# Turning one batch's queries with a DMA transpose instead of TensorE

## The chip, the cores and the metric

The kernel runs on one core of a Trainium2 chip. A core has TensorE (PE: matmuls, with weight loads counted apart as PEld), VectorE (DVE), ScalarE (ACT), GpSimd (POOL) and SyncE (SP), which here only issues DMA transfers. Each engine works through its own instructions in order and waits on semaphores for the others. The metric is the device time of one execution in microseconds (us); the kernel before takes 230.7 us, the median of three runs from 230.65 to 230.78.

## The reference, cut to what matters

Attention over keys and values that are averaged in groups of eight, then a maxout layer and an output matmul. There are 8 batches, 8 heads, 576 positions and 64 channels a head; 4608 tokens of 512 channels enter the second part.

```python
k_p = k.reshape(B, H, Sp, 8, D).mean(axis=3)       # 72 pooled keys per head
v_p = v.reshape(B, H, Sp, 8, D).mean(axis=3)
scores = scale * np.matmul(q, k_p.transpose(0, 1, 3, 2))
attn = softmax(scores)                             # written out in the reference
x = np.matmul(attn, v_p)                           # -> (B*S, H*D), heads side by side
h = np.maximum(np.maximum(x @ w1, x @ w2), x @ w3)
out = h @ w_out
```

## The kernel before

The kernel interleaves the attention of batch b with the matmuls of the second part for tokens that are already there. The second part goes in blocks of 512 tokens. A block is a list of short pieces of TensorE work, its slots: first the hidden layer (`hidden`), then the output (`project`, two slots for 128 tokens each). After each slot a plan can insert steps of a batch's attention. Batches are counted from 0, so "the third batch" is batch 2.

The steps that matter here:

```python
# loads, issued by GpSimd; the pool ld has two buffers for each of q, k and v
    def after(loads, first):          # the loads also wait for this instruction
        ...
    def load_q(b):
        qbs[b] = ld.tile([128, 4, NG, D], BF16, name="qb", tag="qb")
        src = q[b].rearrange("h s d -> (h s d)").rearrange(
            "(hp p t d) -> p hp t d", hp=4, p=128, t=NG)
        n = 2 if b == 0 else 4
        for i in range(0, 4, n):
            nc.gpsimd.dma_start(out=qbs[b][:, i:i + n], in_=src[:, i:i + n])

# adding up groups of eight keys or values on GpSimd (or VectorE)
    def fold(e, t, out, dtype=F32):
        part, n = t.shape[:2]
        f = const.tile([part, n, 4, D], dtype, name="half" if dtype == F32 else "halfh",
                       tag="half" if dtype == F32 else "k16")
        e.tensor_tensor(out=f, in0=t[:, :, 0:4, :], in1=t[:, :, 4:8, :], op=ALU.add)
        e.tensor_tensor(out=f[:, :, 0:2, :], in0=f[:, :, 0:2, :], in1=f[:, :, 2:4, :],
                        op=ALU.add)
        e.tensor_tensor(out=out, in0=f[:, :, 0, :], in1=f[:, :, 1, :], op=ALU.add)

# turning queries on TensorE: transposes into PSUM (tag TR has one buffer), then a copy
    def turn_q(b, n0, n1, evac, tag):
        if b not in qTs:
            qTs[b] = sb2.tile([128, 2 * NG, 128], BF16, name="qT", tag="qT")
        pqt = psum([128, n1 - n0, 128], BF16, name="pqt", tag=tag[0],
                       bufs=tag[1])
        qf = qbs[b].rearrange("p hp t d -> p (hp t d)")
        for n in range(n0, n1):
            nc.tensor.transpose(pqt[:, n - n0, :], qf[:, 128 * n:128 * n + 128],
                                ident)
        evac(out=qTs[b][:, n0:n1, :], in_=pqt)

# turning keys: three transposes, then four copies that spread the heads into the kz tiles
    def turn_k(b):
        pkt = keys(b, ATT if len(pools) < 3 else SC)
        for par, evac in enumerate((nc.vector.tensor_copy, nc.scalar.copy)):
            for odd in range(2):
                (evac if b > 2 else nc.vector.tensor_copy)(
                    out=kz_all[b % 2][par][64 * par:64 * par + 64, :, 0:Sp].rearrange(
                         "p h (r i t) -> p h r i t", i=3, t=2)[:, :, :, :, odd],
                     in_=pkt[64 * odd:64 * odd + 64].rearrange("p i (h r) -> p h r i", r=12))

    def do(b, steps):                 # the plan's steps, by letter
            if name[0] in "qQ":       # a quarter of the queries, by TensorE
                turn_q(b, *QS[i], ... nc.scalar.copy, TR)    # QS: 5, 5, 4 and 4 transposes
            elif name[0] == "T":      # all queries of a batch, by one DMA transpose
                qTs[b] = sb2.tile([128, 2 * NG, 128], BF16, name="qT", tag="qT")
                nc.sync.dma_start_transpose(
                    out=qTs[b], in_=qbs[b].rearrange("p hp t d -> p (hp t d)"))
            elif name[0] == "k":
                turn_k(b)
            elif name[0] == "s": ...  # scores of head i: two matmuls (even and odd kz), then exp
            elif name[0] == "v": ...  # attention times values for a chunk of tokens
            elif name[0] == "x": ...  # turning the result into xT
```

The hidden layer's pieces take three PSUM buffers in turn. Of two pieces the first is read by ScalarE (`t`), the second by VectorE (`hT`, the maximum of both). Blocks 0 and 1 begin with twelve half-width pieces (slots 0 to 11); from slot 12 on they are 512 wide.

```python
    def hidden_part(n, jc, c0, c1, hT):
        col = slice(NB * n + c0, NB * n + c1)
        for wi in range(1, 3):
            pw = psum([128, c1 - c0], F32, name=f"pw{wi}", tag="pw", bufs=3)
            for kc in range(KCH):
                mm = nc.tensor.matmul(pw, w_sb[wi][:, kc, bass.ts(jc, 128)],
                                      xT[:, kc, col],
                                      start=(kc == 0), stop=(kc == KCH - 1))
            mms.append(mm)
            if wi == 1:
                t = sb2.tile([128, c1 - c0], F16, name="t0", tag="t0")
                nc.scalar.activation(out=t, in_=pw, func=FT.Relu)
            else:
                nc.vector.tensor_tensor(out=hT[:, jc, c0:c1], in0=t, in1=pw,
                                        op=ALU.max)
            yield
```

The output's pieces end in a copy on ScalarE into `osb` (five buffers) and two stores issued by SP:

```python
# [cut from project(n): matmuls with wm and wo]
                    nc.scalar.copy(out=osb[:, c], in_=po)
                for u in range(2):
                    b, g = divmod(2 * m + u, NG)
                    dst = out[S * b:S * b + S, :].rearrange("(r g) c -> r g c", g=NG)
                    (nc.scalar if last and u else nc.sync).dma_start(
                        out=dst[:, GS[g], c], in_=osb[64 * u:64 * u + 64, c])
```

Block 0, what GpSimd gets after it, block 1's plan, and what GpSimd gets at its first slot:

```python
    def block(n, plan, parts, folds=()):

        for slot, _ in enumerate(part for stage in parts for part in stage(n)):
            if slot == 0 and n > 0:
                pool_work(n, mms[-1])
            for b, steps in plan.get(slot, ()):
                if b < B:
                    do(b, steps)
            if folds and slot in FOLDS:
                next(folds.pop(0))

    fold_v(1)
    block(0, {0: [(0, "v2")], 1: [(0, "v3")], 3: [(0, "x2 x3 w1 v4")], 6: [(0, "x4 d1")], 9: [(0, "w2")], 10: [(0, "d2")], 11: [(0, "w3")], 12: [(0, "w4")], 14: [(0, "w5 z")],
              17: [(1, "K")], 24: [(1, "q0 k")], 25: [(1, "q1")],
              26: [(1, "s0 q2")], 27: [(1, "s1 s2")], 28: [(1, "s3 Q3")],
              29: [(1, "s4 s5")], 30: [(1, "s6 s7")], 31: [(1, "v0")],
              32: [(1, "v1 x0")], 33: [(1, "X1 v2 v3")]}, (hidden, project))
    load_k(3, nc.gpsimd)
    load_v(3, nc.gpsimd)
    load_q(3)
    fold_k(2, nc.gpsimd)
    fold_v(2)

    def plan1():
        return {1: [(1, "x2")], 2: [(1, "v4")], 3: [(1, "x3")],
                5: [(1, "x4")],
                6: [(2, "k")], 7: [(2, "q0")], 9: [(2, "q1")], 11: [(2, "q2 s0")],
                12: [(2, "s1 q3")], 13: [(2, "s2")], 14: [(2, "s3")], 15: [(2, "s4"), (3, "T")],
                16: [(2, "s5")], 18: [(2, "s7")],
                19: [(2, "v0")],
                20: [(2, "v1 x0")], 21: [(2, "v2 x1")], 22: [(2, "v3 x2")],
                23: [(2, "v4 x3")], 24: [(2, "x4"), (4, "T")], 17: [(2, "s6")]}

# [cut: plan(n) for the later blocks, with "T" two batches ahead]
    FOLDS_OF = {1: "k3 v3", 2: "k4 v4 k5", 3: "v5 k6 v6", 4: "k7 v7"}

    def pool_work(n, mm):

        if n + 3 < B:
            if n == 1:
                load_q(4)
            after([load_k(n + 3, nc.gpsimd)], mm)
            load_v(n + 3, nc.gpsimd)
            if n > 1:
                load_q(n + 3)
        for name in FOLDS_OF.get(n, "").split():
            if name[0] == "k":
                fold_k(int(name[1]), nc.gpsimd)
            else:
                fold_v(int(name[1]))
```

So batches 0, 1 and 2 have their queries turned by TensorE, batches 3 to 7 by a DMA transpose that SP issues. `load_q(4)` stands ahead of the folds of batch 3 in GpSimd's order.

Of the kernel before, what the change touches and what calls it, by code (L numbers as in the profile page):

```python
# [14 lines left out]
def kernel(  # L15
# [11 lines left out]
    nc = tc.nc  # L27
# [37 lines left out]
    kts, vts, qbs, kps, qTs, ets = {}, {}, {}, {}, {}, {}  # L65

    def after(loads, first):
        for x in loads:
            tc.add_manual_dep(x.ins, first.ins.name, mybir.DependencyInfo(
                mybir.DependencyClass.Sync, mybir.DependencyReason.DATA),  # L70
                reason="weights first")
# [22 lines left out]
    def load_q(b):  # L94
        qbs[b] = ld.tile([128, 4, NG, D], BF16, name="qb", tag="qb")
        src = q[b].rearrange("h s d -> (h s d)").rearrange(
            "(hp p t d) -> p hp t d", hp=4, p=128, t=NG)
        n = 2 if b == 0 else 4
        for i in range(0, 4, n):
            nc.gpsimd.dma_start(out=qbs[b][:, i:i + n], in_=src[:, i:i + n])  # L100

    w_sb = [const.tile([128, KCH, DFF], F16, name=f"mw{wi}", tag=f"mw{wi}")
            for wi in range(3)]
# [19 lines left out]
    for sign in (1, -1):  # L123
        nc.gpsimd.affine_select(
            out=pick, in_=pick, compare_op=ALU.is_ge, fill=0.0, base=7 * (sign < 0),
            pattern=[[sign, 6], [-8 * sign, 128]], channel_multiplier=6 * sign)
    for i in range(3):
        load_w(slice(256 * i, 256 * i + 256))
    nc.gpsimd.dma_start(
        out=wo_sb, in_=moe_w_out.rearrange("(jc p) c -> p jc c", p=128))  # L130
# [25 lines left out]
    def new_kp(b):  # L156
        kps[b] = sb2.tile([96, 6, D], BF16, name="kp", tag="kp")

    def fold_k(b, e, i0=0, i1=6):
        if b not in kps:  # L160
            new_kp(b)
        fold(e, kts[b][:, i0:i1], kps[b][:, i0:i1], F16 if e is nc.vector else F32)

    def fold_v(b):
        fold(nc.gpsimd, vts[b], vp_all[:, b, :, 0:D])
# [48 lines left out]
    def new_et(b):  # L214
        ets[b] = sb2.tile([Sp, H, S], F16, name="et", tag="et")
# [20 lines left out]
    def turn_x(b, c0, keep, xn, tag, evac=nc.scalar.copy):  # L236
        if b > 2:
            g0 = S * b + c0
            nc.sync.dma_start_transpose(
                out=xT[:, :, g0 + keep:g0 + 128],  # L240
                in_=xn.rearrange("p g h d -> p (g h d)")[keep:128])
            return
        pxt = psum([128, KCH, 128], F16, name="pxt", tag=tag[0], bufs=tag[1])
        for kc in range(KCH):
            nc.tensor.transpose(
                pxt[:, kc, :],
                xn[:, kc // 2, 2 * (kc % 2):2 * (kc % 2) + 2, :], identh)
        g0 = S * b + c0
        evac(out=xT[:, :, g0 + keep:g0 + 128], in_=pxt[:, :, keep:128])  # L249
# [23 lines left out]
    PW = ("pw", 3)  # L273

    QS = ((0, 5), (5, 10), (10, 14), (14, 18))
    xns, mms = {}, []

    def do(b, steps):

        for name in steps.split():
            i = int(name[1:] or 0)
            if name[0] in "qQ":
                turn_q(b, *QS[i], nc.vector.tensor_copy if name[0] == "Q"
                       else nc.scalar.copy, TR)
            elif name[0] == "T":
                qTs[b] = sb2.tile([128, 2 * NG, 128], BF16, name="qT", tag="qT")
                nc.sync.dma_start_transpose(
                    out=qTs[b], in_=qbs[b].rearrange("p hp t d -> p (hp t d)"))  # L290
            elif name[0] == "k":
                turn_k(b)
            elif name[0] == "K":
                fold_k(b, nc.vector)
            elif name[0] == "s":
                if i == 0:
                    new_et(b)
                (scores if len(pools) < 3 else scores_flat)(b, i)
            elif name[0] == "d":
                sub_w(i)  # L300
            elif name[0] == "z":
                for par in range(2):
                    nc.vector.memset(kz_all[1][par], 0.0)
            elif name[0] == "w":
                turn_w(i, nc.scalar.copy if i % 2 else nc.vector.tensor_copy)
            elif name[0] == "v":
                xns[b, i] = values(b, CHUNKS[i][0])
            else:
                turn_x(b, *CHUNKS[i], xns[b, i], TR if b == 1 else ATT,
                       nc.vector.tensor_copy if name[0] == "X" else nc.scalar.copy)  # L310
# [4 lines left out]
    def sub_w(i, j0=0, j1=2, wi=(1, 2)):  # L315

        part = slice(256 * i + 128 * j0, 256 * i + 128 * j1)
        for t in [w_sb[w] for w in wi]:
            nc.vector.tensor_tensor(out=t[:, :, part], in0=t[:, :, part],  # L319
                                    in1=w_sb[0][:, :, part], op=ALU.subtract)  # L320

    def turn_w(jc, evac):
        pwt = psum([128, KCH, 128], F16, name="pwt", tag=TR[0], bufs=TR[1])
        for kc in range(KCH):
            nc.tensor.transpose(pwt[:, kc, :], w_sb[0][:, kc, bass.ts(jc, 128)], identh)
        evac(out=w1T[:, jc, :], in_=pwt.rearrange("p k c -> p (k c)"))
# [171 lines left out]
    def block(n, plan, parts, folds=()):  # L498

        for slot, _ in enumerate(part for stage in parts for part in stage(n)):  # L500
            if slot == 0 and n > 0:
                pool_work(n, mms[-1])
            for b, steps in plan.get(slot, ()):
                if b < B:
# [9 lines left out]
              32: [(1, "v1 x0")], 33: [(1, "X1 v2 v3")]}, (hidden, project))  # L514
    load_k(3, nc.gpsimd)
    load_v(3, nc.gpsimd)
    load_q(3)
    fold_k(2, nc.gpsimd)
    fold_v(2)


    def plan1():
        return {1: [(1, "x2")], 2: [(1, "v4")], 3: [(1, "x3")],
                5: [(1, "x4")],
                6: [(2, "k")], 7: [(2, "q0")], 9: [(2, "q1")], 11: [(2, "q2 s0")],
                12: [(2, "s1 q3")], 13: [(2, "s2")], 14: [(2, "s3")], 15: [(2, "s4"), (3, "T")],
                16: [(2, "s5")], 18: [(2, "s7")],
                19: [(2, "v0")],
                20: [(2, "v1 x0")], 21: [(2, "v2 x1")], 22: [(2, "v3 x2")],
                23: [(2, "v4 x3")], 24: [(2, "x4"), (4, "T")], 17: [(2, "s6")]}  # L530
# [11 lines left out]
    def pool_work(n, mm):  # L542

        if n + 3 < B:
            if n == 1:
                load_q(4)
            after([load_k(n + 3, nc.gpsimd)], mm)
            load_v(n + 3, nc.gpsimd)
            if n > 1:
# [293 lines left out]
```

The softmax here doesn't subtract the row's maximum and nothing guards it: scores larger than these inputs give would overflow.

## Time and profile before

| what | before |
|---|---|
| time, median of three runs | 230.7 us |
| span of the profiled run | 229.0 us |
| TensorE busy | 219.8 us |
| GpSimd busy | 140.0 us |
| block 1, start to end on TensorE | 51.45 to 77.51 us |
| query transposes by TensorE (L182) | 54, 219 ns long in the median |
| query transposes by DMA (L289) | 5, landing 3.9 to 7.4 us after issue |

Times in the profile are us from the start of the span. A line such as "56.00 0.44 PE L182 MATMUL pqt<-ident,qb ... x5" gives start, length, engine, line of the kernel, operation, result and operands, and how many instructions were merged. Square brackets tell how long the engine was idle before, and what released it. Matmuls overlap in the pipeline, so a group's cost is read from the starts.

### The profile page before, as it was taken

Reading aid. Unit: us, or ns where it says so; the run is one execution under the profiler, and the core shown is the slowest. Engines: PE = TensorE matmul, PEld = TensorE weight load, DVE = VectorE, ACT = ScalarE, POOL = GpSimd, SP = SyncE. Lnnn points to the kernel's source line nnn. Section 1 sums busy time; section 2 is a strip of 40 time slices with the busy share of each in tenths; the row PEclk is TensorE's granted clock in tenths of the full one; section 3 lists DMA queues with packets and bytes.
Section 4 is the critical chain, followed back from the end, with each engine's and each line's share of the span. In section 5 each row is a group of like instructions: output and inputs, shape, how many; then the busy total and the mean of one; then the engine's idle time right before and its main releaser. Section 6 shows DMA issues by size and latency. Waiting matters only on the chain.

```text
span 229.0 us, 4411 instructions
## 1 busy us (share of the span) xinstructions
PE 219.8 (96%) x1686; PEld 134.9 (59%) x1687; DVE 130.5 (57%) x246; ACT 122.6 (54%) x221; POOL 140.0 (61%) x115
## 2 busy tenths in 40 slices
PE   7888999999999999999999999999999999999992
PEld 2477645568655545544554455455677667786682
DVE  3668876048426423632363236368578887897830
ACT  2277425756864586238623852683776435465330
POOL 7975201999959999999999759900343443920020
PEclk9999999999999999999999999999999999999999
DMA  6999999999569999986998799941421534301326
GB/s 172 208 197 197 211 202 208 194 177 225 106 110 216 221 161 212 159 194 119 223 153 199 127 218 189 190 110 24 92 53 40 121 71 87 84 11 46 76 68 183
DMA packets 47157, 33.52 MB, mean 146 GB/s; under 512 B 27104, under 2 KB 41888, under 8 KB 47136
## 3 DMA queue, kind: packets, MB, share of 16 engines
q0 software_dynamic: 16944, 16.98, 46.0%
q1 hardware_dynamic: 30032, 16.13, 32.2%
q8 instruction: 13, 0.21, 0.4%
q10 hardware_dynamic: 160, 0.13, 0.2%
q14 instruction: 8, 0.07, 0.1%
HBM read 34.60 MB, written 9.44 MB: 192 GB/s over the span
## 4 chain that ended last, share of the span: by engine, by line
PE 88%; DVE 6%; ACT 3%; issue 2%; DVEq 0%; ACTq 0%
PE pw L346 23%; PE po L395 18%; PE po L391 11%; PE pA L733 7%; PE psc L207 6%; PE pav L255 4%; PE pC L733 3%; PE wm L413 3%; PE pm L333 2%; PE oA L670 2%; PE pB L733 2%; DVE kz L198 2%; PE pqt L182 2%; DVE xn L263 2%; ACT kz L198 2%
## 5 line engine op out<-in xcount | busy, mean ns | idle before, releaser
L346 PE MATMUL pw<-xT,mw 128*128 128x512 f16 (+1 forms) x336 | 73.1, 349 | 0.4 <-ACT xT L249 0.2
L395 PE MATMUL po<-mwo,hT 128*128 128x512 f16 (+1 forms) x198 | 46.8, 373 | 0.0
L354 DVE TENSOR_TENSOR hT<-t,pw 128x512 f16<-128x512 f16 (+1 forms) x42 | 25.5, 610 | 36.7 <-ACT et L212 22.3
L346 PEld LDWEIGHTS <-mw 128*128 128x128 f16 x336 | 31.6, 98 | 21.5 <-DVE mw L319 0.6
L400 ACT COPY osb<-po 128x512 f32<-128x512 f32 (+1 forms) x32 | 18.5, 579 | 41.2 <-PE po L395 41.1
L212 ACT ACTIVATE et<-psc 72x576 f16<-72x576 f32 (+2 forms) x54 | 35.2, 660 | 7.1 <-PE psc L207 6.9
L151 POOL TENSOR_TENSOR half<-vt 72x2048 f32<-72x2048 f16 x7 | 28.4, 4060 | 14.1 <-DMA vt<-in_v_dram 13.7
L391 PE MATMUL po<-wm,xT 128*128 128x512 f16 (+1 forms) x132 | 33.0, 372 | 0.3 <-ACT osb L400 0.3
L352 ACT ACTIVATE t<-pw 128x512 f16<-128x512 f32 (+1 forms) x42 | 22.5, 537 | 13.4 <-PE pw L346 11.6
L263 DVE TENSOR_TENSOR xn<-pav,rcp 128x512 f16<-128x512 f32 x40 | 27.7, 691 | 1.6 <-DVE rcp L261 0.2
L395 PEld LDWEIGHTS <-hT 128*128 128x128 f16 x198 | 18.5, 98 | 16.3
L152 POOL TENSOR_TENSOR half<-half 72x1024 f32<-72x1024 f32 (+1 forms) x13 | 27.3, 2097 | 1.0
L207 PE MATMUL psc<-qT,kz 128*128 128x320 bf16 (+2 forms) x120 | 22.9, 278 | 1.8 <-DVE qT L184 0.9
L207 PEld LDWEIGHTS <-kz 128*128 128x128 bf16 x143 | 13.1, 98 | 14.7 <-ACT kz L198 2.0
L151 POOL TENSOR_TENSOR half<-ktFalse 96x1536 f32<-96x1536 f16 x6 | 18.6, 3099 | 4.3 <-DMA ktFalse<-in_k_dram 4.1
L255 PEld LDWEIGHTS <-et 72*128 72x128 f16 x320 | 15.4, 98 | 7.6 <-issue 0.3
L739 ACT CAST pad<-pA 128x512 f16<-128x512 f32 x27 | 15.3, 587 | 8.4 <-PE pA L733 6.0
L261 DVE RECIPROCAL rcp<-pav 128x8 f32<-128x8 f32 x40 | 8.2, 206 | 18.1 <-PE pav L255 17.9
L391 PEld LDWEIGHTS <-xT 128*128 128x128 f16 x132 | 12.1, 98 | 9.4 <-issue 0.4
L255 PE MATMUL pav<-vp,et 72*128 72x65 f16 x320 | 17.0, 194 | 0.1
L714 DVE SCALAR_TENSOR_TENSOR hT<-pad 128x512 f16<-128x512 f16 x18 | 14.4, 810 | 1.8 <-ACT pad L743 1.4
L733 PEld LDWEIGHTS <-sw 128*128 128x128 f16 x144 | 13.7, 98 | 2.7
(106 smaller groups left out, 279.2 us busy)
## 6 DMA issues: line engine op xcount, KB each, us to landing
out_dram<-osb SPq DMA_DIRECT2D x62, 128.0 KB, 3.2
ktFalse<-in_k_dram POOLq DMA_DIRECT2D x7, 576.0 KB, 6.6
qb<-in_q_dram POOLq DMA_DIRECT2D x7, 576.0 KB, 13.2
vt<-in_v_dram POOLq DMA_DIRECT2D x7, 576.0 KB, 10.9
mw<-in_moe_w_dram POOLq DMA_DIRECT2D x9, 256.0 KB, 9.2
ktTrue<-in_k_dram SPq DMA_DIRECT2D x3, 384.0 KB, 5.0
mwo<-in_moe_w_out_dram POOLq DMA_DIRECT2D x1, 768.0 KB, 13.2
qb<-in_q_dram POOLq DMA_DIRECT2D x2, 288.0 KB, 7.8
```

The source lines that it names most:

```text
L151: e.tensor_tensor(out=f, in0=t[:, :, 0:4, :], in1=t[:, :, 4:8, :], op=ALU.add)
L152: e.tensor_tensor(out=f[:, :, 0:2, :], in0=f[:, :, 0:2, :], in1=f[:, :, 2:4, :], op=ALU.add)
L207: nc.tensor.matmul(out, kz_all[b % 2][f % 2][:, h, :], qTs[b][:, n + i0:n + i1, 64 * (h % 2):64 * (h % 2) + 64], start=True, stop=True)
L212: nc.scalar.activation(out=out, in_=in_, func=FT.Exp, scale=1.0 / 64.0)
L255: nc.tensor.matmul(pav[:, h // 4, 65 * (h % 4):65 * (h % 4) + 65], ets[b][:, h, c0:c0 + 128], vp_all[:, b, h, :], start=True, stop=True)
L263: nc.vector.tensor_tensor(out=xn, in0=pv[:, :, :, 0:D], in1=rcp.to_broadcast([128, 2, 4, D]), op=ALU.mult)
L346: mm = nc.tensor.matmul(pw, w_sb[wi][:, kc, bass.ts(jc, 128)], xT[:, kc, col], start=(kc == 0), stop=(kc == KCH - 1))
L352: nc.scalar.activation(out=t, in_=pw, func=FT.Relu)
L354: nc.vector.tensor_tensor(out=hT[:, jc, c0:c1], in0=t, in1=pw, op=ALU.max)
L391: nc.tensor.matmul(po, xT[:, kc, bass.ts(m, 128)], wm_sb[:, kc, c], start=(kc == 0), stop=False)
L395: nc.tensor.matmul(po, hT[:, jc, bass.ts(mm, 128)], wo_sb[:, jc, c], start=False, stop=(jc == JCH - 1))
L733: mm = nc.tensor.matmul(p[:, w], a[:, kc, bass.ts(g, 128)], b[:, kc, :], start=(i in FIRST and w + kc == 0), stop=(w + kc == 2), skip_grou ...
```

## The change

Batch 2's queries are turned by a DMA transpose as well. SP issues it in block 0 at slot 32, between the stores of the third and of the fourth 128 tokens, so that it is there before block 1 needs it in slot 11. The steps `q0` to `q3` leave block 1, and the key step moves from slot 6 to slot 7. So that no other transfer is in the way, the loads of batch 3 are put behind batch 2's key fold, the query load first, and wait for the transpose. In the same way the query load of batch 4 waits for the transpose of batch 3; the call that gives GpSimd its work in block 1 moves from slot 0 to slot 16, because that transpose is issued at slot 15.

```diff
@@ load_q
-        for i in range(0, 4, n):
-            nc.gpsimd.dma_start(out=qbs[b][:, i:i + n], in_=src[:, i:i + n])
+        return [nc.gpsimd.dma_start(out=qbs[b][:, i:i + n], in_=src[:, i:i + n])
+                for i in range(0, 4, n)][-1]
@@ do
-                nc.sync.dma_start_transpose(
+                turned[b] = nc.sync.dma_start_transpose(
@@ block
-            if slot == 0 and n > 0:
+            if slot == (16 if n == 1 else 0) and n > 0:
                 pool_work(n, mms[-1])
@@ block 0
-              32: [(1, "v1 x0")], 33: [(1, "X1 v2 v3")]}, (hidden, project))
+              32: [(2, "T"), (1, "v1 x0")], 33: [(1, "X1 v2 v3")]}, (hidden, project))
+    fold_k(2, nc.gpsimd)
+    after([load_q(3)], turned[2])
     load_k(3, nc.gpsimd)
     load_v(3, nc.gpsimd)
-    load_q(3)
-    fold_k(2, nc.gpsimd)
     fold_v(2)
@@ plan1
-                6: [(2, "k")], 7: [(2, "q0")], 9: [(2, "q1")], 11: [(2, "q2 s0")],
-                12: [(2, "s1 q3")], 13: [(2, "s2")], 14: [(2, "s3")], 15: [(2, "s4"), (3, "T")],
+                7: [(2, "k")], 11: [(2, "s0")],
+                12: [(2, "s1")], 13: [(2, "s2")], 14: [(2, "s3")], 15: [(2, "s4"), (3, "T")],
@@ pool_work
             if n == 1:
-                load_q(4)
+                after([load_q(4)], turned[3])
```

More of the change, by code (lines that the diff above doesn't have):

```diff
@@ L275 @@
     QS = ((0, 5), (5, 10), (10, 14), (14, 18))
-    xns, mms = {}, []
+    xns, mms, turned = {}, [], {}
     def do(b, steps):
```

## The prediction

> **What bounds the kernel now.** I read the page's busy shares first, then its chain that ended last, then the waits of the weight loads and matmuls, and last the timeline of block 1, which is where the removed work lies.
>
> ```profile
> PE 219.8 (96%) x1686; PEld 134.9 (59%) x1687; DVE 130.5 (57%) x246; ACT 122.6 (54%) x221; POOL 140.0 (61%) x115
> PE 88%; DVE 6%; ACT 3%; issue 2%; DVEq 0%; ACTq 0%
> ```
>
> TensorE is busy 96% of the span and is 88% of the chain that ended last. No transfer stands in that chain. So the time can fall by what leaves TensorE's stream, and can rise by what makes TensorE wait. The waits of TensorE from 30 to 170 us sum to little, and none of them is for a transfer (who waited for whom, us in total, times, the longest):
>
> ```profile
> PE psc L207 <- ACT kz L198: 0.8, 3, 0.3
> PE po L391 <- ACT osb L400: 0.3, 1, 0.3
> ```
>
> Block 1 begins at 51.45 and block 2 at 77.51. The timeline of TensorE at the place that changes (start, length, line, what, count):
>
> ```profile
> 55.43 0.29 PE L189 MATMUL pkt<-ident,kp 96*128 96x96 bf16 x3
> 55.56 0.60 PE L346 MATMUL pw<-xT,mw 128*128 128x256 f16 x4
> 56.00 0.44 PE L182 MATMUL pqt<-ident,qb 128*128 128x128 bf16 x5
> 56.28 1.04 PE L346 MATMUL pw<-xT,mw 128*128 128x256 f16 x8
> 57.22 0.44 PE L182 MATMUL pqt<-ident,qb 128*128 128x128 bf16 x5
> 57.51 1.33 PE L346 MATMUL pw<-xT,mw 128*128 128x256 f16 x8
> 58.67 0.39 PE L182 MATMUL pqt<-ident,qb 128*128 128x128 bf16 x4
> 58.90 0.41 PE L207 MATMUL psc<-qT,kz 128*128 128x320 bf16 x2
> ```
>
> The lengths overlap because matmuls are pipelined; what a group costs is the distance from its start to the next start. One 128x256 group of four costs 56.00 - 55.56 = 0.44. Two such groups should cost 0.87, and do from 56.28, but from 57.51 to 58.67 they cost 1.16: there is a hole of 0.29. The same stretch of the chain names its cause (its times stand some 0.16 later than the timeline's for matmuls), and VectorE's timeline shows it:
>
> ```profile
> 57.76 0.43 DVE hT L354
> 58.20 0.04 issue
> 58.24 0.60 PE pw L346 x4
> ```
> ```profile
> 55.76 1.97 DVE L198 COPY kz<-pkt 64x288 bf16<-64x288 bf16 x4 [0.30 <-PE pkt L189]
> 57.76 0.75 DVE L354 TENSOR_TENSOR hT<-t,pw 128x256 f16<-128x256 f16 x2
> ```
>
> VectorE spreads batch 2's keys into the kz tiles for 1.97 us. The maximum of the part before has to queue behind that, and holds a PSUM buffer which TensorE wants. The reader should keep these four copies in mind: they limit what the change can give.
>
> **What the Trainium skill says.** "TensorE: Matmul & The Clock Gate", Part 4: PE-mode transpose, says that a 128x128 transpose is a matmul against the identity and that its result lands in PSUM, so a copy must follow; it gives about 275 ns within a kernel. The trace has 219 ns of length, but in a run of five the starts are 0.28 / 5 = 56 ns apart, and that is the cost used here. "DMA: Bandwidth & Descriptors", DMA Transpose (X-bar), says that the plain DMA transpose needs a hardware queue (SP or ACT) and a two-byte type; the five in this trace are on SP and bf16. The same page, Issuing engines are not separate DMA queues, says that transfers of all issuers run on the same 16 DMA engines and interleave. The trace agrees: the query transpose at 61.45, with the DMA idle, landed 4.0 us after its issue, the one at 76.56, among loads and stores, 7.4 us.
>
> **The change part by part.**
>
> Removed from TensorE: 18 transposes (5, 5, 4 and 4). From the starts: 0.28 + 0.29 + 0.23, and 60.47 - 60.25 = 0.22 for the last four, together 1.02 us. A further 0.07 goes with them, the wait of the second group at 57.15 for its single PSUM buffer. Removed from ScalarE: the four copies of them, 2 x 0.69 + 2 x 0.58 = 2.54 us. ScalarE is busy 16.6 of 26.1 us in block 1 and no wait of TensorE in this stretch ends at it, so this counts for nothing.
>
> Moved: the keys' step goes from slot 6 to slot 7. The first use of kz, in slot 11, stays. With the transposes gone only slots 8 to 11 stand between, and this is the term that takes part of the gain back. I walk it from slot 6's start at 54.99, which does not change:
> - Slots 6 and 7 run to 55.86, the key transposes to 55.99. Slots 8 to 11 follow at 0.435 each, to 57.73. Their PSUM buffers are free: the maximum of slot 7 now stands ahead of the copies on VectorE.
> - That maximum waits for ScalarE's slot 6 (55.63 + 0.38) and runs 56.08 to 56.50. The four copies then take 1.97, about 56.42 to 58.39.
> - Slot 11's first score needs only the even kz, ready at about 57.4. It runs 57.73 to 57.87. The second needs the odd kz, ready at 58.39; with 0.08 for the hand-over it starts at about 58.47. TensorE waits 0.60 us.
> - It ends at 58.58. Slot 12 runs to 59.44, the next score to 59.69, and slot 13 starts there.
>
> Before, slot 13 started at 60.47. The gain is 60.47 - 59.69 = 0.78 us; as a sum, 1.02 + 0.07 + 0.29 (old hole) - 0.60 (new hole) = 0.78. From slot 13 to block 2 the stream of before has no hole, so the 0.78 should be carried to the end.
>
> Added: one DMA transpose on SP in block 0, behind six of its eight stores. Those six are issued by about 49.5. SP is held for 2.0 us (the median is 2.03), the result should land about 4 us after issue, at 53.6, and the first score needs it at 57.7. The last two stores go out at about 51.6 instead of 51.35. There are five osb buffers and the next store is at 69, so that costs nothing. The queries, loaded since 22.08, are there: the longest landing of any query load is 20.3 us.
>
> Moved on GpSimd: batch 2's key fold goes ahead of batch 3's loads. It took 49.26 to 55.34 and now starts at about 47.1, so its result is there at about 53.2, well before 55.86. The queries' load of batch 3 then waits for the transpose, to about 54.1; the three loads take 2.2 us to issue, and the value fold of 7.8 us ends at about 64.1. That result is needed at slot 19, about 67.6. Then the loads of batch 4 wait for the transpose of batch 3. Its queries now lead the loads, and land perhaps at 60; the transpose then runs beside k and v and may need up to 7.4 us as the one at 76.56 did, so it lands at 64 to 67.4. Before, GpSimd resumed at 65.96. It had the keys of batch 3 folded at 74.2; they are needed at 78.38 - 0.78 = 77.6. Nothing on TensorE's path moves unless that transpose lands after about 69.
>
> Sum: 230.7 - 0.78 = 229.9 us. I round the estimate up to 230.0, since every uncertain step can only cost.
>
> **The rivals.**
> - The whole removed work is gained: 1.02 plus both small holes, 1.4 us, giving 229.3. For it: a stream without holes everywhere else. Against it: the 1.97 us of copies, which now start after slot 7 and must end before slot 11's second score. It would need those copies to be faster.
> - The transpose of batch 3 takes the place of the removed wait: it lands at 69 or later behind batch 3's key and value loads, the key fold of batch 3 comes late, and block 2's key transposes wait. 230.2 to 231.5. For it: 7.4 against 4.0 us when there was traffic, and GpSimd idle 2.71 us at just this wait before. Against it: over 3 us of slack at 74.2 against 77.6.
> - The new transpose lands late, after 57.7, and the first score waits. 230.5 to 232. For it: stores and the last load of v share the engines at 49 us. Against it: three loads that filled the DMA from 47 us on now start after it, and 4 us of slack.
> - Nothing at all: block 1 turns out bound elsewhere, 230.7. Against it: TensorE is busy 25.93 of its 26.06 us.
>
> **The range and the chances.** The main line has about 7 in 10, the full gain 1 in 10, the two late transposes 2 in 10 together, mostly with small losses. That gives 230.0 with 229.4 to 230.7. Two per cent is 4.6 us, over four times the work removed, so faster by 2% is all but excluded; slower by 2% would need a transfer to stall TensorE by over 5 us. Chances: 0.01, 0.97, 0.02.
>
> **What would show each step right or wrong.** The removal: 36 transposes of queries instead of 54 on TensorE, and block 2 starting about 0.8 us earlier than 77.51. The new hole: in slot 11 the two scores of the first head lie about 0.6 us apart beyond the usual, released by VectorE's last kz copy, and the old hole before slot 11 is gone. The transfer: a sixth query transpose on SP near 49.5, landing in about 4 us, with no wait of a score for it. GpSimd: the key fold of batch 2 near 47, and the loads of batch 4 issued near 66. The prediction is wrong if block 2's key transposes or a value product waits for GpSimd, if a score waits for the transpose, or if the scores of slot 11 don't wait for VectorE at all.

## The result and the profile after

The changed kernel takes 234.55 us (median of 5, 234.52 to 235.31), the kernel before 230.65 us in the same measurement. The ratio is 1.018 with an interval of 1.016 to 1.020: it is slower by 1.8%. Ratios here leave disturbed executions out, so where executions scatter a ratio can differ from that of the two medians.

The page's busy shares and its chain by engine, of the changed kernel:

```profile
PE 220.1 (94%) x1668; PEld 133.8 (57%) x1669; DVE 130.1 (56%) x246; ACT 120.6 (52%) x217; POOL 140.9 (60%) x115
PE 75%; DMA 8%; DVE 5%; POOL 4%; ACT 3%; issue 2%; DVEq 0%; POOLq 0%; ACTq 0%
```

TensorE has 18 matmuls fewer and is busy a little longer; transfers and GpSimd, absent from the chain before, now hold 12% of it. TensorE's waits from 30 to 170 us (us in total, times, the longest):

```profile
PE pkt L189 <- POOL kp L154: 1.9, 1, 1.9
PE pw L346 <- ACT osb L400: 1.0, 1, 1.0
PE psc L207 <- ACT kz L198: 0.5, 2, 0.3
PE psc L207 <- DVE kz L198: 0.5, 1, 0.5
PE po L391 <- ACT osb L400: 0.3, 1, 0.3
```

The first two are new and far from block 1. A table of starts on TensorE, read from both timelines, tells where the time goes:

| TensorE starts | before | after | difference | step |
|---|---|---|---|---|
| block 1 | 51.45 | 51.79 | +0.34 | |
| block 2 | 77.51 | 77.11 | -0.40 | -0.74 |
| block 2, key transposes of batch 3 | 78.38 | 80.06 | +1.68 | +2.08 |
| block 2, slot 3 | 80.92 | 83.85 | +2.93 | +1.25 |
| block 3 | 100.35 | 104.46 | +4.11 | +1.18 |
| first product of the last tokens | 214.90 | 219.22 | +4.32 | +0.21 |

The steps add to 3.98 us; with the 0.34 us from before block 1 that is the 4.32 of the last row. These are two profiled executions, of 235.30 and 230.77 us; the median of the changed kernel lies 0.75 us below the profiled one. So block 1 gains what was meant to be gained, and block 2 of the profiled execution loses six times as much in three pieces.

**The gain.** TensorE and then VectorE in block 1 of the changed kernel:

```profile
56.21 0.29 PE L189 MATMUL pkt<-ident,kp 96*128 96x96 bf16 x3
56.34 1.91 PE L346 MATMUL pw<-xT,mw 128*128 128x256 f16 x16
58.09 0.30 PE L207 MATMUL psc<-qT,kz 128*128 128x320 bf16 x1
58.85 0.28 PE L207 MATMUL psc<-qT,kz 128*128 128x256 bf16 x1 [0.46 <-DVE kz L198]
```
```profile
56.82 1.97 DVE L198 COPY kz<-pkt 64x288 bf16<-64x288 bf16 x4
58.82 0.75 DVE L354 TENSOR_TENSOR hT<-t,pw 128x256 f16<-128x256 f16 x2
```

The four slots follow without a hole (56.34 + 4 x 0.44 = 58.09). The second score starts 0.76 after the first instead of 0.14, when the copies end.

**The loss.** The chain of the changed kernel from block 1 into block 2 (start, us, what):

```profile
60.24 0.31 PE pw L346 x2
60.55 10.64 DMA qT<-qb
...
71.75 0.79 POOL qb L99
72.54 0.14 POOL ktFalse L79
...
73.95 3.10 POOL half L151
...
77.13 1.80 POOL half L152
...
79.01 1.00 POOL kp L154
...
80.06 0.30 PE pkt L189 x3
```

This reads backwards from 80.06: the key transposes of batch 3 wait for their fold on GpSimd; the fold starts only after batch 4's loads are issued; the first of these waits for the query transpose of batch 3, which was issued at 60.55 and took 10.64 us. GpSimd shows that wait in brackets:

```profile
63.50 1.26 POOL L154 TENSOR_TENSOR vp<-half 72x512 f16<-72x512 f32 x1
71.75 0.79 POOL L99 DMA_DIRECT2D qb<-in_q_dram  x1 [6.98 <-DMA qT<-qb]
```

Why 10.64? The DMA queues from 58 to 68 us, first of the kernel before, then of the changed one (q0 carries GpSimd's loads, q1 SP's stores and transposes; packets, MB, share of the engines):

```profile
q0 software_dynamic: 402, 0.45, 31.7%
q1 hardware_dynamic: 2336, 0.59, 26.0%
```
```profile
q0 software_dynamic: 1223, 1.55, 91.5%
q1 hardware_dynamic: 518, 0.13, 29.4%
```

Before, batch 3's loads were issued from 47.09 and had all landed by 61.3, just as the transpose was issued at 61.45. Now they are issued from 54.72 and the last of them lands at 56.04 + 13.4 = 69.4. The transpose lands 1.8 us after that. In the ten microseconds shown, q1 moved 0.13 MB, little of the transpose; most of its packets came from 68 us on.

TensorE's timeline where it waits shows the second piece:

```profile
77.11 1.03 PE L346 MATMUL pw<-xT,mw 128*128 128x512 f16 x4
80.06 0.30 PE L189 MATMUL pkt<-ident,kp 96*128 96x96 bf16 x3 [1.92 <-POOL kp L154]
80.20 3.41 PE L346 MATMUL pw<-xT,mw 128*128 128x512 f16 x8
83.41 0.61 PE L207 MATMUL psc<-qT,kz 128*128 128x320 bf16 x2
```

Eight 512-wide matmuls take 3.41 where they took 1.89 in the kernel before (at 78.50): after the idle time the granted clock is 0.5 (0.57 on average from 80 to 84 us, 1.00 before and after). That costs 1.5 us; the step is 1.25 because the hole of 0.27 before the second score is gone. This piece is not in the median: 4 us at 0.57 lower the mean clock of the span by 0.007 (4 x 0.43 / 233.6), and the two executions of 235.3 us have a mean clock of 0.993, while the three of 234.5 us have 0.998 to 1.0. None of those three was profiled.

The third piece, at 104.46, is for the tokens of x that the DMA turns in block 2. The list of TensorE's waits above puts it down to ScalarE's copy into `osb`, which was done at 104.08; TensorE's weight loads name the transpose in their own list of waits ("DMA xT<-xn: 1.5"). The two transposes of x issued from 98.20 landed in 5.2 us, in the kernel before in 2.7. The experiments below bear out the transposes.

### The profile page after: what moved, and what is told of

Its sections match the earlier page's. It is cut to its first block, busy times and chain, and to the rows that moved or that the text cites. A ratio compares the mean times of both kernels' runs of the same rounds, so it can differ in the third digit from the quotient of the medians.

```text
span 233.6 us, 4375 instructions
## 1 busy us (share of the span) xinstructions
PE 220.1 (94%) x1668; PEld 133.8 (57%) x1669; DVE 130.1 (56%) x246; ACT 120.6 (52%) x217; POOL 140.9 (60%) x115
## 4 chain that ended last, share of the span: by engine, by line
PE 75%; DMA 8%; DVE 5%; POOL 4%; ACT 3%; issue 2%; DVEq 0%; POOLq 0%; ACTq 0%
PE pw L346 22%; PE po L395 15%; PE po L391 10%; PE pA L733 6%; DMA qT<-qb 5%; PE psc L207 4%; DMA vt<-in_v_dram 4%; PE pav L255 3%; PE pC L733 3%; PE pm L333 2%; PE oA L670 2%; PE pB L733 2%; DVE kz L198 2%; DVE xn L263 2%; POOL half L151 1%
## 5 line engine op out<-in xcount | busy, mean ns | idle before, releaser
L346 PE MATMUL pw<-xT,mw 128*128 128x512 f16 (+1 forms) x336 | 74.2, 354 | 1.4 <-ACT osb L400 1.0
L198 DVE COPY kz<-pkt 64x288 bf16<-64x288 bf16 x18 | 8.6, 479 | 14.1 <-PE pkt L189 13.9
## 6 DMA issues: line engine op xcount, KB each, us to landing
vt<-in_v_dram POOLq DMA_DIRECT2D x7, 576.0 KB, 13.4
```

## The experiments

Theory A was that all of the loss enters through one place, GpSimd's wait for a transpose that loads in flight delay. Rivals: the new transpose itself, GpSimd's new order, and the late loads acting on other transposes.

**Without the wait of batch 4's load.**

```diff
-                after([load_q(4)], turned[3])
+                load_q(4)
```

> The change without the wait of batch 4's query load for batch 3's transpose; everything else stays. Theory A (the loss comes through GpSimd, which sat 6.98 us at this wait and so folded batch 3's keys too late): GpSimd goes on at about 64.8, the keys are folded at about 73, TensorE doesn't wait for them, the clock stays up, 229.8 to 230.3 us. Theory B (the transpose of batch 3 is itself too late when loads are in flight, whoever waits for it): with three more loads beside it it lands after 75, possibly after the first score of batch 3 at about 79.5 wants it, and the time stays above 232 us.

230.32 us, ratio to the kernel before 0.9972 (0.9962 to 0.9981): the one line is worth 4.2 us (234.55 - 230.32; the kernel before took 230.65 and 230.94 in the two measurements). GpSimd issues the load at 64.66 without waiting and has the keys folded at 72.9. All waits of TensorE from 45 to 170 us:

```profile
PE psc L207 <- ACT kz L198: 0.8, 3, 0.3
PE psc L207 <- DVE kz L198: 0.5, 1, 0.5
PE po L391 <- ACT osb L400: 0.3, 1, 0.3
```

Both new waits are gone. The transpose itself got slower, 11.8 us, but lands near 73, well before its first use near 80. So its lateness did no harm directly; the engine put behind it did. Theory B falls. The trace of the kernel before puts a wait of 2.71 us at this load down to the same transpose, though the line isn't there; that transpose landed at 65.45 (61.45 + 4.0), and the wait cost nothing. What makes such a wait dear is how late the transfer lands.

**Batch 3's loads after its transpose.**

```diff
-    load_k(3, nc.gpsimd)
-    load_v(3, nc.gpsimd)
     fold_v(2)
@@ pool_work, block 1
-                after([load_q(4)], turned[3])
+                after([load_k(3, nc.gpsimd)], turned[3])
+                load_v(3, nc.gpsimd)
+                load_q(4)
```

> The change with batch 3's key and value loads held back until batch 3's transpose has landed; only its query load is ahead of it. If loads in flight are what makes the transpose late, it now lands 4 to 4.5 us after its issue near 60.5 instead of 10.6, and the time is 230 to 231.5 us (the key fold comes at about 76, just in time). If the transpose is late for another reason (the stores, the new transpose before it), it stays above 8 us and the time above 234 us.

The transpose, with SP's and TensorE's lines below, now takes SP 1.82 us and lands in 3.9:

```profile
60.52 1.82 SPq L289 DMA_TRANSPOSE qT<-qb  x1
```
```profile
102.90 1.02 PE L346 MATMUL pw<-xT,mw 128*128 128x512 f16 x4 [3.28 <-DMA xT<-xn]
```

So the loads in flight are what made it late. The time, 234.30 us (ratio 1.0134, 1.0107 to 1.0162), missed my expectation: batch 3's key and value loads are now issued at 65.02, together with batch 4's, and TensorE waits at block 3 for transposes of x. That is a wait of the kind of the third piece, and larger; which of the moved loads causes it was not tried. The profiled execution, 233.52 us, is the fastest of four.

**Kept warm.**

```diff
+            if n == 2 and slot == 0:
+                hw = psum([128, 512], F32, name="hw", tag=TR[0], bufs=TR[1])
+                for _ in range(9):
+                    nc.tensor.matmul(hw, warm[:, 0:128], warm, start=True, stop=True)
```

> The change with nine extra 128x128x512 matmuls of constants, 1.96 us, on TensorE right where it waits in block 2 before the key transposes; their result is used by nobody. If the lower granted clock after that wait is a consequence of the idle time, the clock stays at 1.0 and about 1.2 us come back: 233.2 to 233.5 us. If it has another cause, 234.5 us or more.

```profile
77.51 2.10 PE L506 MATMUL hw<-warm 128*128 128x512 bf16 x9
79.45 0.29 PE L189 MATMUL pkt<-ident,kp 96*128 96x96 bf16 x3
79.58 1.89 PE L346 MATMUL pw<-xT,mw 128*128 128x512 f16 x8
```

TensorE's timeline shows the clock held: the eight matmuls take 1.89 again. By its mean it also held in three executions of the changed kernel, so this alone doesn't show that the idle time lowers it. The time is 234.84 us, nothing gained. The chain shows why:

```profile
96.32 7.01 DMA xT<-xn
103.33 0.73 issue
104.06 1.02 PE pw L346 x4
```

TensorE arrives earlier and waits 2.47 us at block 3 instead. The transposes are issued 1.88 us earlier than in the changed kernel (96.32 against 98.20), but block 3 starts only 0.40 earlier (104.06 against 104.46): what was won before it is lost to a limit set by transfers.

**Two loads left out.** As the kernel kept warm; batch 5 takes the queries and values of batch 4, so its part of the output is another one.

```diff
+            if n == 2:
+                vts[5], qbs[5] = vts[4], qbs[4]
+            else:
-            load_v(n + 3, nc.gpsimd)
+                load_v(n + 3, nc.gpsimd)
-            if n > 1:
+            if n > 2:
                 load_q(n + 3)
```

> As the kernel kept warm by nine extra matmuls (234.84 us), with the query and value loads of batch 5 left out; batch 5 takes batch 4's queries and values, so its part of the output is another. If TensorE's wait of 2.47 us at the start of block 3 is for transposes of x that stand behind batch 5's late loads, it vanishes: 232.2 to 232.7 us. If that wait has another cause, 234.5 to 235 us.

```profile
100.08 1.46 PE L395 MATMUL po<-mwo,hT 128*128 128x512 f16 x6
101.38 1.03 PE L346 MATMUL pw<-xT,mw 128*128 128x512 f16 x4
```

Block 3 now starts at once (100.08 + 6 x 0.216 = 101.38). The transposes of x issued there land in 3.0 us instead of 6.6. The time is 233.08 us; part of the 2.4 us is lost again at block 5, where a wait of 1.2 us for a transpose of x appears. With this the third piece is shown for the kernel kept warm: batch 5's loads, issued there at 87.06 since GpSimd is late (87.85 in the changed kernel, 82.05 in the kernel before), meet the transposes of x.

**GpSimd's order alone.** The kernel before, its queries still turned by TensorE, with GpSimd's side of the change.

```diff
+    fold_k(2, nc.gpsimd)
+    load_q(3)
     load_k(3, nc.gpsimd)
     load_v(3, nc.gpsimd)
-    load_q(3)
-    fold_k(2, nc.gpsimd)
     fold_v(2)
# also: pool_work at slot 16, load_q(4) after turned[3]
```

> The kernel before with only GpSimd's side of the change: batch 2's key fold ahead of batch 3's loads, the query load first, GpSimd's work of block 1 called at slot 16, the load of batch 4's queries waiting for batch 3's transpose. Batch 2's queries are still turned by TensorE, and nothing waits for a new transpose. If the loss lies in the order of GpSimd's work, the transpose of batch 3 lands near 70, and the time is 232.5 to 234.5 us. If the new transpose itself costs the time, it is 230.7 us.

233.70 us, ratio 1.0134 (1.0098 to 1.0169). The transpose of batch 3 takes 10.3 us and GpSimd waits 7.2. No new transpose exists here, so the loss isn't the new transpose's. Its path differs from the changed kernel's: the keys of batch 3 are folded just in time, the key transposes start at 78.52 (78.38 before), and the clock stays at 1.00. TensorE waits at the starts of blocks 3, 4 and 5 instead; the first and the last of these:

```profile
101.44 1.02 PE L346 MATMUL pw<-xT,mw 128*128 128x512 f16 x4 [0.78 <-ACT osb L400]
148.82 1.02 PE L346 MATMUL pw<-xT,mw 128*128 128x512 f16 x4 [1.04 <-DMA xT<-xn]
```

At the first, too, the weight loads name the transpose ("DMA xT<-xn: 1.2"). The first product of the last tokens starts at 217.57, 2.67 us later than before, and all but 0.14 of that comes after the key transposes. So most of this loss comes through the transposes of x, without any wait for keys.

**The old order with the new transpose.** The change with GpSimd's loads of batch 3 back ahead of the fold, and without both added waits.

```diff
-    fold_k(2, nc.gpsimd)
-    after([load_q(3)], turned[2])
     load_k(3, nc.gpsimd)
     load_v(3, nc.gpsimd)
+    load_q(3)
+    fold_k(2, nc.gpsimd)
     fold_v(2)
# also: pool_work at slot 0, load_q(4) without the wait
```

> The new transpose of batch 2 in block 0 and block 1's new plan, but GpSimd's work in the old order: batch 3's key, value and query loads at about 47, ahead of batch 2's key fold, and no load waits for a transpose by an added dependency. If a transpose lands only when loads in flight have drained, batch 2's transpose, issued near 50 into three loads, lands near 61 to 64 and the first score of batch 2, wanted at 57.7, waits 3 to 6 us: above 233 us. If transposes suffer little from loads, this is 229.8 to 230.5 us.

```profile
64.20 0.64 PE L207 MATMUL psc<-qT,kz 128*128 128x320 bf16 x2 [4.77 <-DMA qT<-qb]
```

238.87 us (1.0338, 1.0300 to 1.0377). The new transpose, issued at 51.22 into three loads, lands 12.9 us later and the first score of batch 2 waits. A good part of the rest of the 8 us is the clock, 0.56 from 64 to 70 us: an estimate of 2.6 us (0.44 x 6). So moving batch 3's loads back was needed; the wait of batch 4's load was not.

**Batch 3's key fold on VectorE.**

```diff
-    FOLDS_OF = {1: "k3 v3", ...
+    FOLDS_OF = {1: "v3", ...
@@ plan1
-     17: [(2, "s6")]}
+     17: [(2, "s6"), (3, "K")]}
```

> The change with batch 3's key fold moved from GpSimd to VectorE at slot 17 of block 1; GpSimd still waits for the transpose. Theory A: the transpose still lands at about 71 and GpSimd still waits about 7 us, but nothing on TensorE hangs on it; 229.8 to 230.3 us, no wait of the key transposes in block 2. Theory C (the late loads of batch 4 alone do the damage, by pushing the DMA transposes of x in block 2): 1 to 1.5 us of the loss stays, 231 to 231.7 us.

It should have freed TensorE from GpSimd, and it did; yet it took 247.12 us (four executions, 244.4 to 250.7; ratio 1.059, 1.056 to 1.063). TensorE's line, and the DMA in stretches (the last two columns are the DMA share and GB/s), from the execution of 250.69 us:

```profile
117.98 1.86 PE L346 MATMUL pw<-xT,mw 128*128 128x512 f16 x4 [18.12 <-DMA xT<-xn]
```
```profile
72.00:80.00 8.00, 7.87 (x62) 3.98 (x59) 3.60 (x8) 4.10 (x9) 7.88 (x5) 1.00 0.99 189
80.00:90.00 10.00, 9.86 (x53) 5.14 (x54) 2.75 (x4) 7.79 (x14) 9.46 (x8) 1.00 1.31 133
90.00:100.00 10.00, 9.85 (x80) 4.97 (x78) 5.18 (x11) 1.87 (x4) 7.50 (x3) 1.00 1.24 78
```

With the fold gone, GpSimd issued batch 5's loads at 81.27, while batch 4's transpose of 77.76 was still under way. It landed after 32.0 us, and the DMA, busy all along, moved 78 GB/s. Neither theory foresaw this.

**The same with batch 5's loads held** until batch 4's transpose has landed:

```diff
+            if n == 2:
+                after([lk], turned[4])      # lk: batch 5's key load
```

> As the kernel with batch 3's key fold on VectorE (247 us), with batch 5's loads also held back until batch 4's transpose has landed. If that transpose, 32 us from issue to landing there, is slow because batch 5's loads are issued while it is still under way, it now lands within about 11 us of its issue near 77.8, TensorE's wait of 18 us at block 3 shrinks to a few us, and the time falls to 231 to 236 us. If it is slow for another reason, the time stays above 243 us.

Batch 4's transpose lands in 10.8 us instead of 32.0, and 247.12 becomes 238.86 us (1.0336, 1.0307 to 1.0364). The mechanism is as expected; the time is 3 us above what I allowed, because the held loads, issued at 89.86, now meet the transposes of x (a wait of 6.83 us at block 3).

That loads come while a transpose is under way is not the whole condition. In the kernel without the wait, batch 5's loads were issued at 80.78, batch 4's transpose at 76.13, and it landed in 12.2 us, not in 32. What separates the two cases stays open.

**The copies spread.** From the kernel without the wait, against the new hole of block 1.

```diff
-                5: [(1, "x4")],
-                7: [(2, "k")], 11: [(2, "s0")],
+                4: [(2, "y0")], 5: [(1, "x4"), (2, "y1")],
+                6: [(2, "y2")], 8: [(2, "y3")], 11: [(2, "s0")],
# y0: key transposes and first copy; y1 to y3: one copy each
```

> As the kernel without the wait of batch 4's query load (230.32 us), with batch 2's key transposes at slot 4 and the four copies into kz one by one after slots 4, 5, 6 and 8 instead of all after slot 7. If the four copies in a row make the new hole of 0.46 to 0.6 us before slot 11's second score, the hole goes and 0.3 to 0.5 us come off against that kernel: 229.8 to 230.0 us. If the copies aren't what limits, 230.3 us.

229.99 us (229.75 to 230.12), ratio to the kernel before 0.9961 (0.9949 to 0.9974). TensorE's line of the two scores is whole again:

```profile
55.42 3.02 PE L359 MATMUL pw<-xT,mw 128*128 128x256 f16 x24
58.27 0.41 PE L218 MATMUL psc<-qT,kz 128*128 128x320 bf16 x2
```

This version beats both kernels, the kernel before by 0.4%. Against the kernel without the wait its time alone proves little, since the intervals of the two ratios overlap; that the hole is gone stands in the trace.

**Scores one slot later in blocks 2 to 4**, on top of it:

```diff
-        got.update({2 + h: [(b, f"s{h}")] for h in range(H)})
+        got.update({3 + h: [(b, f"s{h}")] for h in range(H)})
```

> As the kernel with the copies spread (229.99 us), with the scores of blocks 2 to 4 moved one slot later (slots 3 to 10 instead of 2 to 9), so that the first of them doesn't come before its keys are copied. TensorE's three holes of about 0.43 us before the second score should go: 228.5 to 229.3 us. If something else is behind those holes, 229.8 to 230.1 us.

229.51 us, ratio 0.9934 (0.9910 to 0.9959), and the holes before the second scores are gone. That is less than I expected, and the interval overlaps that of the version before. And one execution of six took 243.0 us. It is the profiled one: batch 4's transpose, issued at 75.44, was still under way when batch 5's loads came at 80.45, and took 27.1 us. So the version stands at the edge that the VectorE variant fell over. The one with the copies spread has nearly the same times (75.71 and 81.04), yet its transpose took 12.3 us and its six executions stay within 230.12 us; I would keep that one, without calling it safe.

## Why the prediction was wrong

- The gain in block 1 was right: 0.78 predicted, 0.74 measured, the new hole 0.60 predicted and 0.62 measured (58.85 - 58.09 - 0.14). The spread copies show that the hole was theirs.
- The new transpose was right: issued at 50.00, landed in 4.1 us, nobody waited for it.
- The step that failed is batch 3's transpose: "the transpose then runs beside k and v and may need up to 7.4 us as the one at 76.56 did, so it lands at 64 to 67.4". I took one transpose among loads for a bound. It landed at 71.2, after the loads that it stood beside; with these held back it needs 3.9 us. The sum to make was when the loads would land: they were issued 7.6 us later than before, and had needed until 61.3.
- The rival that came true was named, with the right condition ("lands after about 69"), but sized at 230.2 to 231.5 and, with the other late transpose, given 2 in 10. It measured 234.55, because I counted only the wait at the key transposes (2.08 in the profiled execution). The missing term is batch 5's loads, 5.8 us late, against the transposes of x: 1.18 in the profiled execution, 2.47 where the clock held in the kernel kept warm, and nearly all of the 2.67 with GpSimd's order alone. The lower clock (a step of 1.25) belongs to the two slower executions of five; they took 0.8 us more than the others.
- Rounding up by 0.1 us "since every uncertain step can only cost" was no substitute for following GpSimd's lateness on into block 2.

## What to carry to other kernels

When a change delays a queue of loads, add the delay to everything that shares the DMA engines, transposes above all, and follow it until it meets a wait with slack. Don't make an engine that has other work in order wait for a transfer which only one of its later uses needs: here one such wait cost 4.2 us. A tuned kernel whose transposes fall between bursts of loads has an edge; ask how far it is before moving either.

## What the runs showed of the hardware

- A query transpose by DMA landed in 3.9 to 4.2 us with no load in flight. Issued into loads, it landed in 7.4 to 13.6 us in most profiles, also where further loads came before it had landed (12.2 and 12.3 for batch 4's); in two profiles of this last kind it took 27.1 and 32.0. In the case of 32.0 the DMA as a whole slowed to 78 GB/s. How the packets of the two queues share an engine was not tried and stays open.
- In the profiled executions the clock fell to 0.5 after a wait of 1.92 us in the changed kernel, but stayed at 1.0 after one of 3.28 us in the kernel with batch 3's loads held back. The mean clock of the other executions suggests that the same kernel can do either: 0.998 to 1.0 in three of the changed kernel, 0.991 to 0.993 in three with the loads held back. What decides stays open. The Trainium skill, "TensorE: Matmul & The Clock Gate", Why this matters for your kernels, advises no idle gaps over about 3 us; here a shorter one was enough, and a longer one not always.
